# A layernorm, sliding attention and bilinear GLU kernel: one more weight group by seven products, and attention's keys and q loaded from ScalarE's queue

## The chip, the cores and the metric

The kernel runs on one core of one Trainium2 chip. The metric is the device time of one execution in microseconds (us), as the median of several runs; lower is better. A core has TensorE (PE, the matrix products; PEld is its weight load), VectorE (DVE), ScalarE (ACT), GpSimd (POOL) and SyncE (SP). Each engine works through its own queue in order. SP, ACT and POOL can each start DMA transfers from their queue.

## The reference

```python
x = A_x                                            # 1 x 2048 x 640
xn = layernorm(x)
q, k, v = heads(xn @ wqkv)                         # 32 heads of 20
# position s looks at s, s-2, ..., s-14 (8 keys, masked below 0)
s = softmax(q . k / sqrt(20)) @ v,  then @ wo
g = silu(((xn @ w_gate) * (xn @ w_up)) @ w_down)   # 640 -> 1536 -> 640
return x + s * g
```

The code feeds one normalized, transposed x (`xT`) both to q, k, v and to gate and up.

## The kernel before

Everything on TensorE is a product of float32 numbers that are split into a high and a low part; three of the four part products are computed (`ALL3`). ScalarE makes a high part as a copy, and GpSimd or VectorE the low part as a difference (`split`, L112). So each operand that is made on the chip costs one pass on ScalarE and one on GpSimd or VectorE.

**Order of the work.** The order on each engine is that of the Python text; it is written out by hand. First come x, its norm and its transpose into `xT` (4 chunks of 512 positions, each a high and a low part of 5 rows of 128). Between these stand the products for q, k, v of the first unit and gate and up of weight groups 0 and 1. There are 12 weight groups of 128 columns, f = 0 to 11. For groups 0 and 1 all chunks are computed in the plain form: `gate_up(f, ch)` is 30 products of 512 columns, 15 for gate and 15 for up.

Then q, k, v follow for the rest of the heads (`qkv(m, r, i)`, L426): five sets of heads m = 0 to 4, two residues r, eight row tiles i, 15 products each. The result of a tile goes to a PSUM bank. While attention runs, the banks come from `ring = [q_one, "g", "u"]` (L517): bank q has one buffer, g and u have two each. ScalarE copies the bank out (L448), and every second tile a DMA writes it to `scr` in DRAM (L452), from ScalarE's queue for m > 0 and from SP's for m = 0.

**Attention** (L468) runs beside this on VectorE and GpSimd. It is a Python generator; `advance(budget)` (L623), called behind each piece of TensorE work, emits as much of it as the budget covers (0.38 a head behind each tile of q, k, v; 0.184 a product in the groups). It works through 12 units (heads of a group, residue) in the order of `ORDER`. For each unit VectorE multiplies q by keys (L542) and sums over a head (L549); the softmax follows; and for the values VectorE multiplies (L508) while GpSimd adds (L514). `ahead` (L480) asks for the next unit's keys and q (`load_kq`, L409) from the middle of the unit before, if they have been written, and for its values (`load_kv`, L417) in the unit itself. All of these loads are in SP's queue.

**Seven products.** From group `F_TWO` = 2 to group 10 the plain form is replaced (`group`, L1253). For two chunks at once, gate and up of 4 of the 5 rows are treated as a 2 x 2 block product by Strassen's scheme in Winograd's form, with seven block products in place of eight; the fifth row is added plainly. `group(f, 2)` is for chunks 2 and 3, `group(f, 0, 1)` for chunks 0 and 1. In the order of the code the seven have 6, 9, 6, 9, 6, 9 and 9 matrix products of 512 columns. This takes:
- sums of x: for chunks 2 and 3 by `differences` (L1156), on GpSimd in steps beside q, k, v; for chunks 0 and 1 by `early_sums` and `early_high` (L598, L611), early, stored to DRAM and loaded back by `load_t` and `load_e` (L1145, L1150) from GpSimd's queue;
- sums of weights on GpSimd (`w_add`, L1229), and splits (`w_split`, L1215) into the tiles G, S, R and U, where U is kept in the rear of R's buffer. For group f + 1 they are made while group f runs, at the places listed in `two_places` (L1410). They start from `wf_raw[f + 1]`, loaded by SP (`load_wf`, L178) into one of two buffers `wraw`; the sums `w_sum[f]` use the other.

At the end of q, k, v (L1391 to L1394) the rest of the steps is emitted, R of the first such group is split, and the next group's raw weights are loaded. Then come groups 2 to 10, group 11 with the output projection between its parts, the projection's remaining products, and the down projection (L866).

Of the kernel before, what the change touches and what calls it, by code (L numbers as in the profile page):

```python
# [42 lines left out]
NP = NT // 2  # L43
PAIRS = range(0, W, 2)
PACE = 1.0
VEC = 2
EARLY = 1
GROUP_RATE = 0.184

# [7 lines left out]
def kernel(  # L57
# [120 lines left out]
    def load_wf(f):  # L178
        wf_raw[f] = slot([P, KD, 2, P], F32) if f == 0 else st([P, KD, 2, P], "wraw", 2)
        nc.sync.dma_start(wf_raw[f], wgu[f])  # L180
# [228 lines left out]
    def load_kq(u):  # L409

        c, b = GROUPS[UN[u][0]] * DH, ORDER.index(u) % 2
        view_kv(u, b)
        q_t[u] = st([P, NE, c], "q", 1)
        nc.sync.dma_start(q_t[u], scr[u][:, 0])
        load_kv(u, 0)

    def load_kv(u, a):  # L417

        zero_kv(u, ORDER.index(u) % 2, a)
        nc.sync.dma_start(kv_t[u][:, a, W - 1:, :], scr[u][:, 1 + a])  # L420
        for p0, p1 in ((0, 112), (112, 127)):
            nc.sync.dma_start(kv_t[u][p0 + 1:p1 + 1, a, 0:W - 1, :], scr[u][p0:p1, 1 + a, 1:, :])

    ALL_RUNS = [(a, b, k) for a, b in ALL3 for k in range(KD)]

# [688 lines left out]
    gate_up(0, 2)  # L1114
    trans_q(15)
    low_parts()
    early_high(1)
    for a in range(2):
        nc.sync.dma_start(e_scr[2 + a], xT[3][a][:, 0:2, :].bitcast(F32))
    made.add(0)  # L1120
# [1 line left out]
    for i in range(TPC, NE):  # L1122
        qkv(0, 1, i)
        advance(PACE * 1.9)
    split_wq(1, nc.gpsimd)
    gate_up(1, 2)
    gate_up(0, 3)
    gate_up(1, 3)

    f0, f1 = KF - 2, KF - 1  # L1130
    F_TWO = 2
    tt, tw, steps = {0: [], 2: []}, {}, []
    T_UNIT = {(j, a, k): divmod(n, 3) for n, (j, a, k) in
              enumerate((j, a, k) for k in range(2) for j in ("T1", "T2", "T3") for a in range(2))}
# [10 lines left out]
    def load_t(n):  # L1145

        tt[0].append(slot([P, 3, CH]))
        nc.gpsimd.dma_start(tt[0][n], t_scr[:, 3 * n:3 * n + 3])
# [104 lines left out]
    def group(f, c0=0, second=0):  # L1253

        b = {"A": pt([P, CH], "g", 2), "C": pt([P, CH], "u", 2), "B": q_one}
        kept, later = {}, []
        eng = nc.vector if c0 and f >= VEC else nc.gpsimd

        def hold(j):
            kept[j] = st([P, CH], "gh", 5)  # L1260
            nc.scalar.activation(kept[j], b["ACACABA"[j]], AF.Copy)  # L1261

        def gate_b():
            nc.vector.tensor_add(kept[2], kept[2], b["C"])

        def up_b():
            eng.tensor_add(kept[1], kept[1], kept[4])

        def h_b():
            eng.tensor_mul(kept[2], kept[2], kept[1])  # L1270
            store_h(f, c0 + 1, kept[2])

        def gate_a():
            nc.vector.tensor_add(kept[0], kept[0], b["B"])

        def up_a():
            nc.vector.tensor_mul(kept[0], kept[0], b["A"])
            store_h(f, c0, kept[0])

        if not second:  # L1280
            if not two(f - 1):
                w_split(f, "U")
            w_sum.pop(f, None)
            wf_raw.pop(f)
        for n, j in enumerate((0, 5, 2, 1, 4, 3, 6)):
            y = b["ACACABA"[j]]
            runs = [(w_unit(f, H_IN[j], k)[i], x_in(W_IN[j], l, k, c0)) for i, l in ALL3 for k in range(2)]
            if j in FIVE:
                name, ch = FIVE[j]
                runs += [(w_unit(f, name)[i], xT[c0 + ch][l][:, KD - 1, :]) for i, l in ALL3]  # L1290
            for r, (w, x) in enumerate(runs):
                nc.tensor.matmul(y, w, x, start=j in (0, 1, 5) and r == 0, stop=r == len(runs) - 1,  # L1292
                                 skip_group_check=True)
            if j in (0, 1, 2, 4):
                hold(j)
            finish_piece()
            if (second, n) == (1, 6) and (second, n) in places:
                places.pop((second, n))(f)
            for act in later:
                act()  # L1300
            later = {5: [gate_a], 3: [gate_b, up_b] + [h_b] * (eng is nc.gpsimd)}.get(j, [])
            if j == 6:
                unfinished.extend([up_a] + [h_b] * (eng is nc.vector))
            if (second, n) in places:
                places[second, n](f)
            if (f, second, n) in beside:
                beside[f, second, n]()
            if (second, n) == (0, 0) and f < f1 and f + 1 not in wf_raw:
                load_wf(f + 1)
            advance(PACE * len(runs) * (GROUP_RATE if two(f) else 0.184))  # L1310
# [32 lines left out]

    def first_parts():
        for name in ("S1", "S2", "S3", "d5", "S4"):
            w_add(2, name)
            yield
        w_split(2, "S")
        yield

    steps += [differences(k) for k in range(2)]
# [4 lines left out]
    for m, t in ((m, t) for m in range(1, len(MADE)) for t in range(DIL)):  # L1356
        r = t if m < last else DIL - 1 - t
        begin_unit(m, r)
        heads, broad = MC[m] // DH, m < last and MC[m + 1] > CMAX
        for i in range(NE):  # L1360
            n = t * NE + i
            if m < last and n == 0:
                load_wq(m + 1, ((0, 2), (2, 4)) if broad else ((0, 3), (3, 5)))
            elif m < last and n in BLOCK:
                split_wq(m + 1, nc.gpsimd, (BLOCK.index(n), BLOCK.index(n) + 1))
            elif broad and n == BLOCK[1] + 1:
                load_wq(m + 1, ((4, 5),))
            if (m, r, i) == (last - 1, 1, 6):
                load_wf(2)
            if (m, n) in W_SUMS:  # L1370
                wd_sum(W_SUMS.index((m, n)))
            qkv(m, r, i)
            if m == last and n == NT - 7:
                staged[:] = [y for y in staged if y is not stage_pk[-1]]
            elif m == last and n == NT - 5:
                load_t(0)
            elif m == last and n == NT - 3:
                w_split(2, "G")
            if i == 1:
                finish_piece()  # L1380
            advance(PACE * heads * 0.38)
            paced += RATE[m - 1][t]
            while paced >= 1:
                paced -= 1
                step()
        if (m, r) == (last - 1, 1):
            steps.append(first_parts())
        elif (m, r) == (last, 1):
            for k in range(2):
                last_difference(k)  # L1390
    step(100)  # L1391
    w_split(2, "R")
    w_sum.pop(2)
    load_wf(3)  # L1394
    beside.update({(f0, 0, 5): lambda: advance(1e9), (f0, 1, 0): lambda: begin_last(), (f0, 1, 1): lambda: load_pair(0),
                   (f0, 1, 4): lambda: sums_wo(), (f0, 1, 6): lambda: split_wo(0, nc.vector)})

# [6 lines left out]
    def sums(*names):  # L1404
        return lambda f: w_add(f + 1, *names)

    def splits(*names):
        return lambda f: w_split(f + 1, *names)
# [8 lines left out]
            load_e(1, 0, 0)  # L1417
            load_e(1, 1, 1)

    for f in range(2, f1):  # L1420
        places.clear()
        places.update(two_places)
        if f == F_TWO:
            for n, at in enumerate((0, 2, 3, 4)):
                places[0, at] = lambda f, n=n: load_late(n)
        group(f, 2)
        group(f, 0, 1)
    places.clear()
    beside.update({(f1, 0, 0): lambda: split_wo(1, nc.vector),
                   (f1, 0, 2): lambda: (turn_pair(0), load_pair(1)), (f1, 0, 4): lambda: (hi_pair(0, 0), lo_pair(0, 0)),  # L1430
# [200 lines left out]
```

## Time and profile before

| | |
|---|---|
| median of 3 runs | 736.02 us (735.68 to 736.02) |
| the profiled execution | 736.29 us, of which the span is 734.4 us |
| products on TensorE | 4030 |
| bytes moved by DMA | 143.78 MB, mean 196 GB/s |

By stage, from the trace's table of busy time (us of each engine in a stretch of the span):

| stretch | us | PE | DVE | ACT | POOL |
|---|---|---|---|---|---|
| x, norm, first q, k, v, gate and up | 0 to 85 | 85.0 | 60.6 | 52.1 | 53.0 |
| gate_up(1, 2), (0, 3), (1, 3) | 85 to 105.4 | 20.4 | 19.0 | 5.4 | 9.5 |
| q, k, v of m = 1 to 4 | 105.4 to 272.7 | 167.3 | 142.6 | 49.0 | 139.4 |
| group 2 | 272.7 to 297.2 | 24.5 | 23.5 | 9.0 | 23.1 |
| groups 3 to 10 | 297.2 to 493.1 | 195.9 | 178.8 | 64.2 | 161.7 |
| group 11 and the output projection | 493.1 to 582 | 88.9 | 84.0 | 50.9 | 52.1 |
| down projection and the output | 582 to 734.4 | 148.1 | 118.0 | 71.6 | 11.7 |

In the profile each row names a line of the kernel, an engine, the operation and the tiles (out<-in, without buffer numbers). What stands in brackets behind a row of the timeline is the time for which the engine was idle before it, and what ended that. SPq, ACTq and POOLq are the queues' own instructions, such as the issue of a DMA.

### The profile page before, as it was taken

The numbers are of one execution on the slowest core, as the hardware profiler recorded it, in microseconds if no ns is written. First come the engines' busy times: TensorE is split into PE (matmuls) and PEld (weight loads), VectorE is DVE, ScalarE is ACT, GpSimd is POOL, SyncE is SP. The second block draws the span as 40 slices with busy tenths as digits, with TensorE's granted clock in tenths as the row PEclk, the third lists the DMA queues.
The fourth block names the chain that finished last, engine by engine and source line by source line (L and its number), as shares of the span: only waits on it lengthen the run. The fifth ranks groups of instructions, "written<-read, shape, count | busy, mean of one in ns | idle before, by whom it ended". The sixth has DMA issues, their size and how long they took to land.

```text
span 734.4 us, 11062 instructions
## 1 busy us (share of the span) xinstructions
PE 728.2 (99%) x4030; PEld 666.0 (91%) x4030; DVE 626.5 (85%) x729; ACT 302.2 (41%) x561; POOL 450.5 (61%) x383
## 2 busy tenths in 40 slices
PE   8999999999999999999999999999999999999997
PEld 6989989988999998888888888888999999999997
DVE  7676998798796989899889999969899997777775
ACT  5668312323232333333233322334566664444442
POOL 6159919997779889797879969766644550000000
PEclk9999999999999999999999999999999999999999
DMA  8564588789767669462733542376768965555534
GB/s 325 170 204 158 208 303 300 239 256 257 190 193 164 220 204 323 141 180 87 221 88 105 177 141 68 80 218 183 208 211 241 315 236 194 194 194 194 194 108 143
DMA packets 106148, 143.78 MB, mean 196 GB/s; under 512 B 23048, under 2 KB 75524, under 8 KB 106094
## 3 DMA queue, kind: packets, MB, share of 16 engines
q1 hardware_dynamic: 88366, 121.13, 52.0%
q10 hardware_dynamic: 16000, 12.78, 5.4%
q0 software_dynamic: 1728, 9.18, 5.1%
q8 instruction: 31, 0.51, 0.3%
q14 instruction: 23, 0.19, 0.1%
HBM read 94.40 MB, written 55.67 MB: 204 GB/s over the span
## 4 chain that ended last, share of the span: by engine, by line
PE 98%; DMA 1%; DVE 0%; SPq 0%; ACT 0%; issue 0%
PE g L1292 16%; PE u L1292 11%; PE q L434 11%; PE q L866 9%; PE u L434 8%; PE g L434 8%; PE u L866 6%; PE q L1292 5%; PE u L124 5%; PE g L124 5%; PE q L996 3%; PE g L866 3%; PE e L866 3%; PE u L996 2%; PE e L996 2%; PE g L996 1%
## 5 line engine op out<-in xcount | busy, mean ns | idle before, releaser
L514 POOL TENSOR_TENSOR o<-o,t 128x960 f32<-128x960 f32 (+1 forms) x66 | 133.7, 2025 | 11.3 <-DVE t L508 10.1
L508 DVE TENSOR_TENSOR t<-e,kv 128x960 f32<-128x960 f32 (+1 forms) x96 | 99.6, 1038 | 21.1 <-POOL o L514 21.1
L542 DVE TENSOR_TENSOR t<-q,kv 128x1920 f32<-128x1920 f32 (+1 forms) x48 | 92.4, 1926 | 2.8 <-DMA kv<-qkv_scr 2.7
L549 DVE TENSOR_REDUCE lg<-t 128x96 f32<-128x1920 f32 (+1 forms) x48 | 92.3, 1923 | 0.2
L434 PE MATMUL q<-s,xc 128*128 128x360 f32 (+1 forms) x450 | 82.8, 334 | 0.5 <-DVE lg L272 0.5
L1261 ACT ACTIVATE gh<-g 128x512 f32<-128x512 f32 x57 | 34.2, 600 | 109.0 <-PE g L1292 108.1
L434 PEld LDWEIGHTS q<-s,xc 128*128 128x128 f32 x450 | 74.8, 188 | 4.6 <-DVE lg L272 0.7
L115 POOL TENSOR_TENSOR s<-wraw,s 128x384 fp32r<-128x384 f32 (+6 forms) x57 | 68.0, 1209 | 17.5 <-ACT s L114 17.5
L434 PE MATMUL u<-s,xc 128*128 128x360 f32 (+1 forms) x360 | 65.8, 334 | 0.0
L434 PEld LDWEIGHTS u<-s,xc 128*128 128x128 f32 x360 | 60.3, 188 | 2.3
L434 PE MATMUL g<-s,xc 128*128 128x360 f32 (+1 forms) x330 | 61.5, 337 | 0.0
L434 PEld LDWEIGHTS g<-s,xc 128*128 128x128 f32 x330 | 55.7, 188 | 2.6
L1292 PE MATMUL g<-s,s 128*128 128x512 f32 x228 | 57.9, 389 | 0.0
L1292 PE MATMUL u<-xc,s 128*128 128x512 f32 x228 | 57.9, 389 | 0.0
L866 PE MATMUL q<-xc,s 128*128 128x320 f32 x342 | 55.5, 309 | 0.0
L866 PEld LDWEIGHTS q<-xc,s 128*128 128x128 f32 x342 | 51.5, 188 | 0.0
L1292 PEld LDWEIGHTS g<-s,s 128*128 128x128 f32 x228 | 42.8, 188 | 8.9
L1292 PEld LDWEIGHTS u<-xc,s 128*128 128x128 f32 x228 | 42.8, 188 | 8.9
L114 ACT ACTIVATE s<-wraw 128x384 fp32r<-128x384 f32 (+6 forms) x58 | 32.6, 581 | 29.4 <-PE g L1292 10.2
L1292 PE MATMUL q<-xc,pk 128*128 128x512 f32 x171 | 41.9, 389 | 0.0
L1292 PE MATMUL g<-xc,s 128*128 128x512 f32 x171 | 41.9, 389 | 0.0
L514 POOL TENSOR_TENSOR o<-t 128x960 f32<-128x960 f32 (+1 forms) x11 | 22.1, 2011 | 27.4 <-DVE t L508 22.7
(328 smaller groups left out, 1559.7 us busy)
## 6 DMA issues: line engine op xcount, KB each, us to landing
h_scr<-gh SPq DMA_DIRECT2D x48, 256.0 KB, 2.8
wraw<-in_wgu SPq DMA_DIRECT2D x11, 640.0 KB, 4.8
kv<-qkv_scr SPq DMA_DIRECT2D x14, 480.0 KB, 6.1
t<-h_scr SPq DMA_DIRECT2D x8, 768.0 KB, 6.3
qkv_scr<-s ACTq DMA_DIRECT2D x17, 360.0 KB, 4.4
kv<-qkv_scr SPq DMA_DIRECT2D x14, 367.5 KB, 7.1
s_scr<-gh SPq DMA_DIRECT2D x16, 320.0 KB, 3.6
gh<-s_scr SPq DMA_DIRECT2D x16, 320.0 KB, 4.1
```

The costliest lines, as they stand in the source:

```text
L114: nc.scalar.activation(hi, raw, AF.Copy)
L115: eng.tensor_sub(lo, raw, hi.bitcast(F32))
L124: nc.tensor.matmul(acc, a, b, start=first and n == 0, stop=last and n == len(runs) - 1)
L434: nc.tensor.matmul(p, xT[(r * NE + i) // TPC][a][:, k, t0:t0 + P], wq[m][b][k], start=n == 0, stop=n == len(runs) - 1, skip_group_check=ac ...
L508: nc.vector.tensor_mul(t.rearrange("p (n d) -> p n d", d=DH), e[:, :, w].unsqueeze(2).to_broadcast([P, NE * nh, DH]), v)
L514: return NE * c * cost, lambda: eng.tensor_add(y, z, t)
L542: nc.vector.tensor_mul(t, q, k)
L549: nc.vector.tensor_reduce(out=lg[:, :, j:j + 2].rearrange("p n a -> p a n"), in_=t.rearrange("p a (n d) -> p a n d", d=DH), op=ALU.add, ax ...
L866: nc.tensor.matmul(p, y[:, i, k], wd_part(name, k, l), start=new and r == 0, stop=r == len(runs) - 1, skip_group_check=True)
L996: nc.tensor.matmul(b, y, w, start=new and r == 0, stop=r == len(runs) - 1, skip_group_check=True)
L1261: nc.scalar.activation(kept[j], b["ACACABA"[j]], AF.Copy)
L1292: nc.tensor.matmul(y, w, x, start=j in (0, 1, 5) and r == 0, stop=r == len(runs) - 1, skip_group_check=True)
```

## The change

- `F_TWO` goes from 2 to 1 and `VEC` from 2 to 1. Chunks 2 and 3 of group 1 are no longer computed by gate_up(1, 2) and gate_up(1, 3); `group(1, 2)` does it, as the first of the groups. Chunks 0 and 1 of group 1 stay in the plain form.
- The raw weights of group 1 are loaded a second time, and the weight sums and splits that were made for group 2 beside q, k, v are now made for group 1. Those of group 2 are made within `group(1, 2)`, at the places of `one_places`, which has them all in one half.
- Keys and q of the next unit are loaded from ScalarE's queue until the end of q, k, v, and from SP's after that. Values stay with SP.
- In the second half of unit (0, 1), behind tile 5: the split of wq for m = 1, the load of wq for m = 2, and `early_high(1)`, in this order. Before, early_high(1) came ahead of tile 4, the split behind tile 7 and the load at the start of m = 1.
- `load_t(0)` and `load_t(1)` move from the last row tiles and group 2 to group 1's first places; `load_t(2)`, `load_t(3)` and `load_e` to places of group 2.
- The pace of attention beside q, k, v goes from 0.38 to 0.39 a head.

```diff
-VEC = 2
+VEC = 1
...
-        nc.sync.dma_start(q_t[u], scr[u][:, 0])
-        load_kv(u, 0)
-
-    def load_kv(u, a):
+        by[0].dma_start(q_t[u], scr[u][:, 0])
+        load_kv(u, 0, by[0])
+
+    by = [nc.scalar]
+
+    def load_kv(u, a, eng=nc.sync):
 
         zero_kv(u, ORDER.index(u) % 2, a)
-        nc.sync.dma_start(kv_t[u][:, a, W - 1:, :], scr[u][:, 1 + a])
+        eng.dma_start(kv_t[u][:, a, W - 1:, :], scr[u][:, 1 + a])
         for p0, p1 in ((0, 112), (112, 127)):
-            nc.sync.dma_start(kv_t[u][p0 + 1:p1 + 1, a, 0:W - 1, :], scr[u][p0:p1, 1 + a, 1:, :])
+            eng.dma_start(kv_t[u][p0 + 1:p1 + 1, a, 0:W - 1, :], scr[u][p0:p1, 1 + a, 1:, :])
...
     gate_up(0, 2)
     trans_q(15)
     low_parts()
-    early_high(1)
...
     for i in range(TPC, NE):
         qkv(0, 1, i)
         advance(PACE * 1.9)
-    split_wq(1, nc.gpsimd)
-    gate_up(1, 2)
+        if i == TPC + 1:
+            split_wq(1, nc.gpsimd)
+            load_wq(2, ((0, 2), (2, 4)))
+            early_high(1)
     gate_up(0, 3)
-    gate_up(1, 3)
+    wf_raw.clear()
 
-    F_TWO = 2
+    F_TWO = 1
...
-            if (second, n) == (1, 6) and (second, n) in places:
+            if n == 6 and (second, n) in places and (second or f == F_TWO):
                 places.pop((second, n))(f)
...
     def first_parts():
         for name in ("S1", "S2", "S3", "d5", "S4"):
-            w_add(2, name)
+            w_add(F_TWO, name)
             yield
-        w_split(2, "S")
+        w_split(F_TWO, "S")
...
-            if m < last and n == 0:
-                load_wq(m + 1, ((0, 2), (2, 4)) if broad else ((0, 3), (3, 5)))
-            elif m < last and n in BLOCK:
+            if 1 < m < last and n == 0:
+                load_wq(m + 1, ((0, 3), (3, 5)))
+            if m < last and n in BLOCK:
...
-                load_wf(2)
+                load_wf(F_TWO)
...
-            elif m == last and n == NT - 5:
-                load_t(0)
             elif m == last and n == NT - 3:
-                w_split(2, "G")
+                w_split(F_TWO, "G")
...
-            advance(PACE * heads * 0.38)
+            advance(PACE * heads * 0.39)
...
+    by[0] = nc.sync
     step(100)
-    w_split(2, "R")
-    w_sum.pop(2)
-    load_wf(3)
+    w_split(F_TWO, "R")
+    w_sum.pop(F_TWO)
+    load_wf(F_TWO + 1)
...
-    for f in range(2, f1):
+    one_places = {(0, 2): splits("G"), (0, 3): sums("S1", "S2", "S3"), (0, 4): splits("S"),
+                  (0, 5): lambda f: (w_add(f + 1, "d5", "S4"), w_split(f + 1, "R")), (0, 6): splits("U")}
+    for f in range(F_TWO, f1):
         places.clear()
-        places.update(two_places)
+        places.update(two_places if f > F_TWO else one_places)
         if f == F_TWO:
-            for n, at in enumerate((0, 2, 3, 4)):
+            places[0, 0] = lambda f: load_t(0)
+            places[0, 1] = lambda f: load_t(1)
+        elif f == F_TWO + 1:
+            for n, at in enumerate((0, 2, 4), 1):
                 places[0, at] = lambda f, n=n: load_late(n)
         group(f, 2)
-        group(f, 0, 1)
+        if f > F_TWO:
+            group(f, 0, 1)
```

## The prediction

> **What bounds the kernel now.** I read the page first, then the waits of TensorE, then the chain of waits in order of time.
>
> ```profile
> span 734.4 us, 11062 instructions
> PE 728.2 (99%) x4030; PEld 666.0 (91%) x4030; DVE 626.5 (85%) x729; ACT 302.2 (41%) x561; POOL 450.5 (61%) x383
> ...
> PE 98%; DMA 1%; DVE 0%; SPq 0%; ACT 0%; issue 0%
> ```
>
> ```profile
> PE q L229 <- POOL lg masks.py:199: 1.4, 1, 1.4
> PE q L434 <- DVE lg L272: 0.5, 1, 0.5
> ```
>
> The span is 734.4 us of an execution of 736.29, so 1.89 us lie around it; the median of the runs shown, 736.02, is 0.27 below this execution. TensorE is busy for 99% of the span, the chain that ended last is TensorE for 98% of it, and TensorE's two waits, for the identity and for the first norm, stand at the very start. So a product less is time less, and any new wait of TensorE is time more. Nothing else counts by itself: the question is only what makes TensorE wait.
>
> ```profile
> 85.17 3.40 PE g L124 x15
> ...
> 478.80 3.40 PE g L1292 x15
> ```
>
> The chain gives the prices: 15 products of 512 columns take 3.40 us, in the plain form (L124) as in the seven-product form (L1292), so 0.2267 us each.
>
> **What is taken away.** gate_up(1, 2) and gate_up(1, 3) are 2 x 30 = 60 products. group(1, 2) is 6+9+6+9+6+9+9 = 54. Six products at 0.2267 are 1.36 us, gained wherever TensorE stays packed. It is also the most that the change can gain, 0.185%. About 0.2% (1.47 us) is what a measurement of this kernel can tell from no change.
>
> **What is moved: the end of unit (0, 1).** Taking out the two gate_ups brings `qkv(1, 0, 0)` 13.6 us forward, to just behind gate_up(0, 3). The keys and q of attention unit 1 are now asked for on ScalarE's queue, in the middle of gate_up(0, 3), right behind ScalarE's copy of the gate. They read what `qkv(0, 1, 7)` wrote to DRAM, and that write stays on SP. So the first question is when it lands; the rows of before around it, from the timeline and the DMA view:
>
> ```profile
> 80.61 1.30 POOL L608 TENSOR_TENSOR kv<-kv,xc 128x512 f32<-128x512 f32 x1
> 81.85 0.61 POOL L616 CAST kv<-kv 128x512 fp32r<-128x512 f32 x1
> 85.00 3.56 PE L124 MATMUL g<-xc,s 128*128 128x512 f32 x15
> 88.35 1.30 POOL L617 TENSOR_TENSOR kv<-kv,t 128x512 fp32r<-128x512 f32 x1
> 89.61 4.39 POOL L115 TENSOR_TENSOR s<-wraw,s 128x1080 fp32r<-128x1080 f32 x3
> 90.09 0.88 SPq L1119 DMA_DIRECT2D e_scr<-xc  x2
> 91.94 1.19 SPq L452 DMA_DIRECT2D qkv_scr<-pk  x1
> 96.41 0.33 SPq L414 DMA_DIRECT2D q<-qkv_scr  x1
> 97.26 0.91 SPq L422 DMA_DIRECT2D kv<-qkv_scr  x2
> 105.40 2.56 PE L434 MATMUL q<-s,xc 128*128 128x360 f32 x15
> 108.00 0.47 ACT L448 ACTIVATE s<-q 128x360 f32<-128x360 f32 x1 [5.20 <-PE q L434]
> 112.60 2.56 PE L434 MATMUL q<-s,xc 128*128 128x360 f32 x15
> ```
>
> ```profile
> qkv_scr<-pk SPq DMA_DIRECT2D x1, 360.0 KB, 4.4
> ```
>
> ```profile
> DMA to landing us min/median/max: 3.0/4.4/12.3
> ```
>
> The second fence is that one write; the third is all the writes of q, k, v (L452) from 85 to 150 us. Step by step:
>
> 1. GpSimd ends the early sums at 81.91 as before. The split of wq(1) (4.39) now comes first, to 86.30; then early_high(1), which took from 81.85 to 89.65 = 7.80, to 94.10.
> 2. SP has early_high's eight stores ahead of the write of `qkv(0, 1, 7)`, so that write goes out at about 94.5 instead of 91.94.
> 3. It landed in 4.4, behind a megabyte of e_scr<-xc and its sister write. Those now go some 10 us earlier, so I take 3.4, nearer to the shortest, 3.0; both ends are kept. Landed: 97.9.
> 4. ScalarE issues the four loads (from 96.41 to 98.17 on SP: 1.76), to 99.7; evacuates `qkv(1, 0, 0)` (0.47, the row at 108.00), to 100.1.
> 5. TensorE is through gate_up(0, 3) at 85.00 + 6.80 = 91.8, fills q, g and u, and wants bank q again three tiles later, as from 105.40 to 112.60, which is 7.2: at 99.0. It stalls 1.1 us; with a landing in 3.0 it is 0.7, in 4.4 it is 2.1. The 12.3 would make it 10, and I leave it out: of the rows it is the furthest from a quiet queue.
>
> That ScalarE does stand still behind a DMA of its own queue is in the trace:
>
> ```profile
> 151.10 4.39 ACTq L452 DMA_DIRECT2D qkv_scr<-pk  x2
> 155.54 0.57 ACT L448 ACTIVATE s<-q 128x480 f32<-128x480 f32 x1 [4.46 <-DMA wraw<-in_wqkv]
> ```
>
> Its two writes held the queue for 4.39 us, and the next evacuation began only at 155.54. The Trainium skill (DMA: Bandwidth & Descriptors, Anatomy of one DMA) says the same of waits: any semaphore wait is spent on the issuing sequencer, before dispatch. Its fit there, 2.0 us plus bytes over 436 GB/s, would land 360 KB in an estimated 2.8 us, for a stall of 0.5 and 0.6 us less in the sum; the trace has nothing under 3.0, and its row is used. Against the change, the skill (Trainium Kernel Development and Optimization, Key Constraints) has it that issuing from several engines saves issue time only.
>
> Later units are safe: by the paces written in the code (an advance of 0.39 a head against 0.38) each next unit was written at least two tiles of q, k, v before its load is asked for, and its loads wait for nothing but 1.8 us of issue on an engine that is busy for 41%.
>
> **What is added: group 1 gets weights of its own form.** wgu[1] is loaded a second time (at nothing: SP asks for it at the place where it asked for wgu[2], two tiles ahead of the first sum), and five sums and four splits are made for it, by the steps that made group 2's. What is new is that group 2's must be made within half a group, mostly by GpSimd:
>
> ```profile
> L514 POOL TENSOR_TENSOR o<-o,t 128x640 f32<-128x640 f32 x24 | 38.2, 1592 | 3.1 <-DVE t L508 2.7
> L115 POOL TENSOR_TENSOR s<-wraw,s 128x384 fp32r<-128x384 f32 x19 | 20.6, 1097 | 0.2 <-ACT s L114 0.2
> L115 POOL TENSOR_TENSOR s<-wraw,s 128x768 fp32r<-128x768 f32 x10 | 18.5, 1855 | 6.8 <-ACT s L114 6.8
> L1238 POOL TENSOR_TENSOR wraw<-wraw 128x256 f32<-128x256 f32 x20 | 18.0, 900 | 14.5 <-DMA wraw<-in_wgu 14.5
> L1238 POOL TENSOR_TENSOR wraw<-wraw,wraw 128x256 f32<-128x256 f32 x20 | 16.1, 803 | 0.5
> L115 POOL TENSOR_TENSOR pk<-wraw,pk 128x640 fp32r<-128x640 f32 x10 | 15.8, 1575 | 3.9 <-ACT pk L114 3.9
> L1238 POOL TENSOR_TENSOR wraw<-wraw 128x128 f32<-128x128 f32 x10 | 6.1, 614 | 0.0
> ```
>
> ```profile
> 109.50 2.27 POOL L514 TENSOR_TENSOR o<-t 128x960 f32<-128x960 f32 x1 [14.80 <-DVE t L508]
> ...
> 272.60 1.52 PE L1292 MATMUL g<-xc,pk 128*128 128x512 f32 x6
> 273.87 0.94 ACT L114 ACTIVATE s<-wraw 128x384 fp32r<-128x384 f32 x2 [0.60 <-ACT s L448]
> 276.24 2.02 POOL L115 TENSOR_TENSOR s<-wraw,s 128x384 fp32r<-128x384 f32 x2
> 277.30 0.35 SPq L180 DMA_DIRECT2D wraw<-in_wgu  x1
> ```
>
> ```profile
> wraw<-in_wgu SPq DMA_DIRECT2D x11, 640.0 KB, 4.8
> ```
>
> The sums of one group are 2 x 0.90 + 2 x 0.80 + 0.61 = 4.02, its splits 1.58 (G) + 1.86 (S) + 2 x 1.10 (R, U) = 5.63: 9.65 us of GpSimd. They can't start before wgu[2] is there, whose buffer comes free with the R split of group 1: in group 2 of before that load went out at 277.30, 4.70 after the group's start at 272.60, and 4.8 later the weights are there: 9.5. That R split came late only because GpSimd was behind; ScalarE's half of it was there at 273.87 + 0.47. Straight behind that, with 1.0 for it, the load goes out 2.9 after the start and lands at 7.7. The last thing made is U, and its low part is wanted by the 30th product of group 2: 12.24 + 29 x 0.2267 = 18.81. So GpSimd has 11.1 us for 9.65, and attention's additions (1.59 each) stand between: with none U is 1.5 early, with one 0.13 late, with two 1.7, with three 3.3; with the load at 9.5, 1.8 more. I take no backlog and one addition, 0.13: GpSimd's one long idle time, 14.80 us before 109.50, now holds the first steps of the sums for chunks 2 and 3, and an addition that is due before 7.7 runs in time which is idle anyhow. Ends for the range: 0 and 3.5.
>
> VectorE gets four passes more for group 1, hidden in its 15% of idle time unless attention's end slips (third rival); ScalarE's extra copies go into its 59%. The first chunks' sums, loaded later, are read in the second half of group 2; the last of them is asked for behind 8.2 us of group 2 and read behind 22.4, and these 14 us hide it unless GpSimd's queue is late by most of them. I put it at nothing.
>
> **The sum.** 736.29 - 1.36 + 1.13 + 0.13 = 736.19 on this execution; 0.27 less for the median: 735.9. That is no change; with a landing in 3.0 or 4.4 this case runs from 735.5 to 736.9.
>
> **The rivals.** (a) No new wait reaches TensorE: the write lands early, or GpSimd is quicker through early_high(1), and U is in time. Then all 1.36 us are kept: 734.7. For it: 0.7 us is a short stall; against it: SP's order of stores before the write is fixed in the code.
> (b) GpSimd has too much in group 1's half: it arrives with group 2's backlog and one addition, or without it and with two, and U is 1.7 to 1.9 late. 735.9 + 1.8 = 737.7, slower; each further addition is 1.6 more. It decides from the second addition on. For it: VectorE starts unit 1 later (its keys are asked for 1.5 us later), so its products and GpSimd's additions come later too.
> (c) VectorE is late at the end of attention:
>
> ```profile
> 478.03 0.68 DVE L1274 TENSOR_TENSOR gh<-gh,q 128x512 f32<-128x512 f32 x1
> ```
>
> Bank q of group 10 is read out at 478.71, and by the chain it is wanted again at 478.80 + 15 x 0.2267 = 482.2: 3.5 us of slack. VectorE's added 2.9 us (estimated: four passes between 0.68 and 1.2 for the group, less two of 0.68 for the plain form) and 1.36 us of earlier products would make it 0.8 late, beside the stall at 99: 736.7.
> That the change does not do what it says can be left out: the count of products is written in the code.
>
> **How the numbers follow.** Forecast 0.35, (a) 0.27, (b) 0.29, (c) 0.09. The bounds of 0.2% are 734.55 and 737.49. (a) stands 0.1 inside the first, and the runs shown lie 0.34 apart: two fifths of it, 0.11, are faster. Slower are (b) and the late ends of the forecast and of (c): 0.36. The rest is the same: 0.53. The range takes in (a) with its scatter, and (b) with one addition more: 734.5 to 739.3.
>
> **What would show it.** TensorE has 4024 products. Right: a gap of about 1.1 us before the fourth tile of m = 1, put down to ScalarE's copy, with ScalarE idle behind loads on its own queue from 89 us; wgu[2] issued about 3 us behind group 1's start; no gap over 0.5 us in group 2. Rival (a): no gap between 85 and 300 us. Rival (b): a gap in group 2's fourth product, put down to GpSimd's split. Wrong altogether: TensorE waits somewhere else, or has a slower product.

## The result

The changed kernel takes 757.69 us (median of 4 runs, 754.39 to 758.49) beside 736.02 for the kernel before: a ratio of 1.0287, with a 95% interval of 1.0256 to 1.0317. The change costs 21.7 us. Its profiled execution took 757.7 us, with a span of 755.9, against 736.29 and 734.4 before.

The page of the changed kernel, the lines that answer to those of before:

```profile
span 755.9 us, 11062 instructions
...
PE 736.1 (97%) x4024; PEld 668.8 (88%) x4024; DVE 622.8 (82%) x731; ACT 305.9 (40%) x568; POOL 457.5 (61%) x392
...
PE 74%; POOL 9%; DMA 7%; DVE 4%; issue 3%; ACT 1%; SPq 1%; ACTq 0%; POOLq 0%; DVEq 0%
```

The six products are gone (4024). But TensorE is no longer the whole chain: a quarter of it now runs over GpSimd, DMAs and VectorE, although none of them became much busier. The waits of TensorE in the changed kernel (total us, how often, the longest):

```profile
PE g L1295 <- ACT gh L1264: 5.9, 3, 3.7
PE g L1295 <- POOL pk L115: 4.3, 2, 3.1
PE q L436 <- ACT s L450: 1.9, 2, 1.0
PE u L1295 <- ACT gh L1264: 1.9, 2, 1.1
```

(L1295 are the groups' products, L1292 before; L436 those of q, k, v, L434 before. L450 and L1264 are ScalarE's copies out of PSUM.) The timeline of TensorE shows where:

```profile
96.09 2.56 PE L436 MATMUL u<-s,xc 128*128 128x360 f32 x15
99.70 2.74 PE L436 MATMUL q<-s,xc 128*128 128x360 f32 x15 [1.04 <-ACT s L450]
102.28 2.63 PE L436 MATMUL g<-s,xc 128*128 128x360 f32 x15
...
115.63 2.74 PE L436 MATMUL q<-s,xc 128*128 128x360 f32 x15 [0.86 <-ACT s L450]
...
263.96 1.55 PE L1295 MATMUL g<-xc,pk 128*128 128x512 f32 x6
...
268.91 1.66 PE L1295 MATMUL g<-s,s 128*128 128x512 f32 x6 [1.33 <-ACT gh L1264]
...
275.09 2.34 PE L1295 MATMUL u<-xc,s 128*128 128x512 f32 x9 [1.12 <-ACT gh L1264]
...
286.60 2.93 PE L1295 MATMUL g<-s,s 128*128 128x512 f32 x6 [3.74 <-ACT gh L1264]
...
313.27 1.20 PE L1295 MATMUL g<-xc,pk 128*128 128x512 f32 x2 [3.05 <-POOL pk L115]
```

A half group is one call of `group`, 54 products; packed, it takes 12.24 us, so the starts of the halves make a ledger. The two gate_ups are gone (60 x 0.2267 = 13.6), and at 85 us this execution was 0.5 ahead of that of before (84.50 for 85.00), so group 1 was due at 272.60 - 13.6 - 0.5 = 258.5.

| where | lost, us | how it comes out |
|---|---|---|
| q, k, v | 5.5 | group 1 starts at 263.96, not 258.5 |
| group 1, and groups 2 and 3 | 13.4 | halves of 15.34, 17.61 and 17.18 (the third is the first half of group 3) |
| halves that start between 387 and 440 | 4.5 | four of 13.50, 12.71, 13.37 and 13.86 |

23.4 lost, less the 1.36 of the products and the lead of 0.5, make 21.5: the difference of the spans.

**In q, k, v.** ScalarE and SP in the changed kernel (ACTq and SPq rows are DMA issues):

```profile
93.99 0.53 SPq L454 DMA_DIRECT2D qkv_scr<-pk  x1
...
96.93 0.35 ACTq L414 DMA_DIRECT2D q<-qkv_scr  x1
...
97.90 1.23 ACTq L424 DMA_DIRECT2D kv<-qkv_scr  x2
99.18 0.47 ACT L450 ACTIVATE s<-q 128x360 f32<-128x360 f32 x1 [10.48 <-PE u L436]
...
100.04 0.58 ACTq L454 DMA_DIRECT2D qkv_scr<-s  x1
...
115.11 0.47 ACT L450 ACTIVATE s<-q 128x360 f32<-128x360 f32 x1 [6.03 <-DMA qkv_scr<-s]
```

The first stall is the predicted one: the write out at 93.99, the loads behind it to 99.13, the copy after them. 99.70 is 1.2 later than the three tiles before allow. The second was not predicted: the write issued at 100.04 landed only after 15.0 us, beside four transfers of w_d of 960 KB each and the load of the next wq, and ScalarE had to wait before it could use the buffer that this write read (6.03 us, the last row). And from 99.70 on each tile of 360 columns takes 2.467 us in place of 2.40, until q, k, v end: 45 x 0.067 = 3.0 us with no wait at all.

**In groups 1 to 3.** GpSimd, ScalarE and SP there:

```profile
266.40 0.99 ACTq L424 DMA_DIRECT2D kv<-qkv_scr  x2
268.85 2.00 POOL L115 TENSOR_TENSOR s<-wraw,s 128x384 fp32r<-128x384 f32 x2
269.90 0.36 SPq L180 DMA_DIRECT2D wraw<-in_wgu  x1
271.43 1.59 POOL L516 TENSOR_TENSOR o<-o,t 128x640 f32<-128x640 f32 x1
273.55 1.56 POOL L516 TENSOR_TENSOR o<-o,t 128x640 f32<-128x640 f32 x1
276.60 0.73 POOL L1241 TENSOR_TENSOR wraw<-wraw 128x256 f32<-128x256 f32 x1
278.80 2.03 POOL L516 TENSOR_TENSOR o<-o,t 128x640 f32<-128x640 f32 x1
284.20 0.94 ACT L114 ACTIVATE s<-wraw 128x384 fp32r<-128x384 f32 x2 [4.47 <-POOL wraw L1241]
285.97 0.58 ACT L1264 ACTIVATE gh<-g 128x512 f32<-128x512 f32 x1
287.25 1.00 POOL L115 TENSOR_TENSOR s<-wraw,s 128x384 fp32r<-128x384 f32 x1
289.11 0.83 SPq L180 DMA_DIRECT2D wraw<-in_wgu  x1
```

wgu[2] is asked for at 269.90, 5.9 us behind the group's start. Its last low part (287.25) ends at 288.2, where the products wanted it at 263.96 + 18.81 = 282.8. Between 265.16 and 287.3 GpSimd has six of attention's additions to do. The first gap, before 268.91, is another matter: from 265.22 to 267.39 ScalarE issues four loads of a next unit's keys and q (266.40 are the last two), and its copy for TensorE comes only behind them and a split, at 268.28. In group 2, ScalarE's copy out of the bank (285.97) stands in the queue behind a split that waited 4.47 us for GpSimd's sums; that is why the trace puts the gap before 286.60 down to ScalarE. Then wgu[3] goes out at 289.11 and takes 13.9 us to land, which makes the gap before 313.27.

### The profile page after: what moved, and what is told of

It is laid out like the page before. It is cut to its first block, busy times and chain, and to the rows that moved or that the text cites. A ratio compares the mean times of both kernels' runs of the same rounds, so it can differ in the third digit from the quotient of the medians.

```text
span 755.9 us, 11062 instructions
## 1 busy us (share of the span) xinstructions
PE 736.1 (97%) x4024; PEld 668.8 (88%) x4024; DVE 622.8 (82%) x731; ACT 305.9 (40%) x568; POOL 457.5 (61%) x392
## 4 chain that ended last, share of the span: by engine, by line
PE 74%; POOL 9%; DMA 7%; DVE 4%; issue 3%; ACT 1%; SPq 1%; ACTq 0%; POOLq 0%; DVEq 0%
PE g L1295 11%; PE q L868 8%; PE q L436 7%; PE u L1295 7%; PE u L436 6%; PE g L436 6%; PE u L868 6%; PE q L1295 4%; PE q L998 3%; PE g L868 3%; PE e L868 3%; DMA wraw<-in_wgu 2%; PE u L998 2%; PE g L124 2%; POOL kv L610 2%
## 5 line engine op out<-in xcount | busy, mean ns | idle before, releaser
L436 PE MATMUL q<-s,xc 128*128 128x360 f32 (+1 forms) x450 | 84.3, 337 | 2.1 <-ACT s L450 1.9
L1264 ACT ACTIVATE gh<-g 128x512 f32<-128x512 f32 x60 | 36.0, 599 | 119.4 <-PE g L1295 117.8
L436 PEld LDWEIGHTS q<-s,xc 128*128 128x128 f32 x450 | 75.6, 188 | 7.0 <-ACT s L450 2.5
L115 POOL TENSOR_TENSOR s<-wraw,s 128x384 fp32r<-128x384 f32 (+6 forms) x60 | 73.1, 1233 | 14.4 <-ACT s L114 14.3
L1295 PE MATMUL g<-s,s 128*128 128x512 f32 x240 | 62.5, 397 | 5.1 <-ACT gh L1264 5.1
L436 PE MATMUL u<-s,xc 128*128 128x360 f32 (+1 forms) x360 | 66.8, 337 | 0.0
L1295 PE MATMUL u<-xc,s 128*128 128x512 f32 x240 | 61.7, 392 | 1.9 <-ACT gh L1264 1.9
L436 PEld LDWEIGHTS u<-s,xc 128*128 128x128 f32 x360 | 61.2, 188 | 2.3
L436 PE MATMUL g<-s,xc 128*128 128x360 f32 (+1 forms) x330 | 62.4, 340 | 0.0
L1295 PEld LDWEIGHTS g<-s,s 128*128 128x128 f32 x240 | 45.7, 191 | 15.4 <-ACT gh L1264 5.9
L436 PEld LDWEIGHTS g<-s,xc 128*128 128x128 f32 x330 | 56.5, 188 | 2.6
L1295 PEld LDWEIGHTS u<-xc,s 128*128 128x128 f32 x240 | 44.8, 188 | 13.0 <-ACT gh L1264 3.1
L114 ACT ACTIVATE s<-wraw 128x384 fp32r<-128x384 f32 (+6 forms) x61 | 34.6, 584 | 48.7 <-issue 12.9
L1295 PE MATMUL q<-xc,pk 128*128 128x512 f32 x180 | 45.3, 397 | 0.0
L1295 PE MATMUL g<-xc,s 128*128 128x512 f32 x180 | 44.2, 390 | 0.8 <-ACT gh L1264 0.8
L1241 POOL TENSOR_TENSOR wraw<-wraw 128x256 f32<-128x256 f32 (+1 forms) x33 | 24.0, 733 | 32.2 <-DMA wraw<-in_wgu 32.2
```

The lines of the kernel that those rows point to most:

```text
L114: nc.scalar.activation(hi, raw, AF.Copy)
L115: eng.tensor_sub(lo, raw, hi.bitcast(F32))
L436: nc.tensor.matmul(p, xT[(r * NE + i) // TPC][a][:, k, t0:t0 + P], wq[m][b][k], start=n == 0, stop=n == len(runs) - 1, skip_group_check=ac ...
L1241: nc.gpsimd.tensor_tensor(v[name], v[a], v[b], op=ALU.add if name == "S1" else ALU.subtract)
```

## The experiments

Two theories stood against each other. **The queue**: ScalarE's in-order queue is what fails; loads and splits that wait stand ahead of copies out of PSUM. **The crowd**: GpSimd has not the time to make group 2's weights in half a group, and whatever queue one relieves, the gap comes back elsewhere. The kernel before, timed beside them, took 735.87 to 736.21. Behind each time stands, in brackets, the 95% interval of its ratio to the kernel before.

**1. Keys and q from SP's queue again, in the changed kernel**

```diff
-    by = [nc.scalar]
+    by = [nc.sync]
```

> The changed kernel with one part undone: keys and q are loaded from SP's queue throughout. Theory A (loads that wait on ScalarE's own queue hold the copies out of PSUM behind them): the stalls before the tiles at 99.70 and 115.63 us (1.2 and 1.0) and the 360-column tiles of 2.467 us in place of 2.40 behind them (45 tiles, 3.0) go, and about 1 us of the stall at 268.91: 757.7 - 6.2 = 751.5, from 750.5 to 753. Theory B (the earlier place of m = 1 is what hurts: the write of the last tile of unit (0, 1) and the DMA traffic are late whatever queue loads): the stalls stay, 756 to 758.

755.25 (1.024 to 1.0283). Both stalls in m = 1 are gone and all its tiles take 2.40, so they did come from ScalarE's queue; the gap in group 1 before its third set of products (268.91 in the changed kernel) is gone too. But TensorE waits 0.72 before 185.57, where ScalarE, by the trace, had waited 8.39 us for one of its own writes, and from there the tiles take 2.467 again: group 1 starts at 262.15, only 1.8 earlier. Groups 1 to 3 lose 11.1. A holds for the place, not for the sum.

**2. The seven products alone**: as run 1, with unit (0, 1) in its old order (early_high(1) ahead of tile 4, the split behind tile 7, the load of wq for m = 2 at the start of m = 1) and the old pace.

```diff
+    early_high(1)
...
-        if i == TPC + 1:
-            split_wq(1, nc.gpsimd)
-            load_wq(2, ((0, 2), (2, 4)))
-            early_high(1)
+    split_wq(1, nc.gpsimd)
...
-            advance(PACE * heads * 0.39)
+            advance(PACE * heads * 0.38)
```

> The kernel before with the seven products for group 1 alone: unit (0, 1) in the old order, keys and q from SP's queue, pace 0.38; group 2's weights made within group 1, and the first chunks' sums loaded at the changed places. Theory A (two separate causes; the one of groups 1 to 3 is the crowded half group: splits on ScalarE that wait for GpSimd's sums, with copies out of PSUM behind them, and wgu[3] late): the gaps of the changed kernel at 268 to 327 us stay, 12 to 16 us, less the 1.4 of the six products: 747 to 751. Theory B (group 1 was late only since attention and the queues came late out of the disturbed q, k, v): no gap over 1.5 us in groups 1 to 3, 735 to 738.

751.08 (1.0171 to 1.0239), at the end of A's range. Groups 1 to 3 lose 11.1 (halves of 19.20, 13.32 and 15.29) with no load on ScalarE's queue, so those loads do not explain them; splits that wait on ScalarE are still there, and run 5 is about these. Group 3 loses 3.0 of the 11.1 although its weights landed in 4.2 us, so their late landing is not the only way to lose there. And q, k, v lose 5.5 here too (group 1 starts at 264.53, where 259.0 was due): TensorE waits 0.47 before 94.09 for GpSimd's split of wq, and from 95.18 on the tiles take 2.467. ScalarE's loads are thus not the only thing that makes q, k, v late at the earlier place.

**3. ScalarE's loads alone, in the kernel before**

```diff
-        nc.sync.dma_start(q_t[u], scr[u][:, 0])
+        by[0].dma_start(q_t[u], scr[u][:, 0])
```

Here `by[0]` is ScalarE's queue until the end of q, k, v, then SP's, for the keys too.

> The kernel before with keys and q loaded from ScalarE's queue until the end of q, k, v, and nothing else. Theory A (a load on ScalarE's queue costs only where its write has not landed when TensorE is about to need ScalarE): at unit 1 two gate and up pieces lie between the write and the next need, no stall over 0.3 us there, 736.0 to 737.0, and the 360-column tiles stay at 2.40. Theory B (any such load delays the copies by its issue of about 2 us, in every unit): stalls at several units and slow tiles behind the first of them, 739 to 742.

744.67 (1.0106 to 1.014), worse than either theory. Nothing happens at unit 1, as A has it, but the unit after it costs one long wait. ScalarE and TensorE in this run:

```profile
129.62 0.63 ACT L1168 ACTIVATE s<-gh 128x512 fp32r<-128x512 f32 x1 [6.94 <-POOL gh L1164]
130.16 0.45 ACT L450 ACTIVATE s<-g 128x360 f32<-128x360 f32 x1
130.64 0.52 ACTq L454 DMA_DIRECT2D qkv_scr<-s  x1
134.91 0.35 ACTq L414 DMA_DIRECT2D q<-qkv_scr  x1
137.27 0.45 ACT L450 ACTIVATE s<-u 128x360 f32<-128x360 f32 x1
138.13 3.77 PE L436 MATMUL q<-s,xc 128*128 128x360 f32 x15 [3.96 <-ACT s L450]
```

The load stands right behind the write that it reads, so ScalarE waits out its landing. They are that close because ScalarE came late to the write: it had waited 6.94 us for one of GpSimd's sums for chunks 2 and 3. The same wait is in the kernel before, where it cost nothing:

```profile
129.19 0.63 ACT L1166 ACTIVATE s<-gh 128x512 fp32r<-128x512 f32 x1 [6.32 <-POOL gh L1162]
```

So ScalarE, at 41%, had no slack at this place. The wait (4.1), the slow restart of the next tiles (1.8) and then 2.467 a tile (30 x 0.067 = 2.0) make the 8 us by which group 2 starts later.

**4. One wait of TensorE, in the kernel before**

```diff
+            for _ in range(12 if (m, r, i) == (1, 0, 0) else 1):
                 nc.scalar.activation(y[...], p..., AF.Copy)
```

> The kernel before, where ScalarE copies the first tile of m = 1 out of its bank twelve times over in place of once (the same values), so that TensorE has to wait once, for about 0.8 us, before the fourth tile; nothing else differs. Theory A (one wait of TensorE leaves the 360-column products in a slower rhythm until products of another kind reset it): all 360-column tiles behind it take 2.467 us, 44 x 0.067 = 2.9 more, so 736.0 + 0.8 + 2.9 = 739.7. Theory B (the slow tiles come from the DMA traffic or from where the operands lie): the tiles go back to 2.40 at once, 736.8.

741.05 (1.0055 to 1.0085): A in kind, and 1.35 more than its number.

```profile
110.15 2.56 PE L434 MATMUL u<-s,xc 128*128 128x360 f32 x15
114.00 2.74 PE L434 MATMUL q<-s,xc 128*128 128x360 f32 x15 [1.29 <-ACT s L449]
116.58 2.63 PE L434 MATMUL g<-s,xc 128*128 128x360 f32 x15
```

The wait of 1.4 us made group 2 start 4.8 later. No DMA was added, and no operand lies elsewhere.

**5. Group 2's high copies by GpSimd, in the changed kernel**

```diff
+            if f == F_TWO + 1:
+                nc.gpsimd.tensor_copy(hi, y)
+                nc.gpsimd.tensor_sub(lo, y, hi.bitcast(F32))
```

> The changed kernel, where the high copies of group 2's splits are made by GpSimd in place of ScalarE; nothing else differs. Theory A (ScalarE's queue: a split that waits for GpSimd's sum or for the load of wgu[2] holds the copies out of PSUM behind it): the gaps before 275.09 and 286.60 us (1.3 and 3.9, both put down to ScalarE's gh) go, and GpSimd, with some 3 us more to do, makes U later by as much, of which 1 to 3 reach TensorE: 757.7 - 5.2 + 2 = 754.5, from 752 to 756. Theory B (GpSimd simply has too little time in the half group, and it does not matter who makes the high parts): the gaps move to GpSimd's low parts and grow by its added work, 758 to 761.

756.79 (1.025 to 1.0289). ScalarE's waits in group 2 are gone, but TensorE's waits have moved:

```profile
PE u L1300 <- POOL s L1232: 2.6, 1, 2.6
PE g L1300 <- ACT gh L1269: 2.1, 2, 1.3
...
PE g L1300 <- POOL s L1232: 1.4, 1, 1.4
```

(L1232 is GpSimd's new copy.) The gap went where B has it: group 2's first half now loses 7.9 in place of 5.4, near the 3 us that GpSimd got to do more. But group 1's half loses 1.7 in place of 3.1, as A has it, and group 3 only 0.8, so that groups 1 to 3 lose 10.3 in place of 13.4; q, k, v were 1.9 later in this execution, and the total hardly moved. So ScalarE's queue has a part in group 1, and in group 2 the gap stays whichever engine makes the high copies.

**6. Without group 2's weights, in the changed kernel**

```diff
-    load_wf(F_TWO + 1)
...
-        places.update(two_places if f > F_TWO else one_places)
+        places.update(two_places if f > F_TWO else {})
```

> The changed kernel without the making of group 2's weights: they are not loaded, summed or split, and group 2 computes with group 1's (so its columns are not those of the reference). Theory A (the crowded half group is the cause of all gaps from 275 to 327 us): those before 275.09 and 286.60 (1.3 and 3.9), the slower clock behind the second (1.3), the late wgu[3] with its gap (3.4) and the slow stretch behind it (1.2) go, 11.1 in all: 757.7 - 11.1 = 746.6, from 745 to 749. Theory B (the gaps come from attention and the queues, which leave q, k, v late): most of them stay, over 752.

747.96 (1.0141 to 1.0171): A. The half of group 1 takes 13.88, and the three behind it 12.24 each. The crowd costs 13.4 - 1.6 = 11.8 us; 2.3 of that was taken back by longer stalls in q, k, v in this execution (group 1 at 266.23). The 1.6 that stay are the gap behind ScalarE's four loads, which run 1 does not have.

**7. The first chunks' sums loaded early, in the changed kernel**

```diff
+            elif m == last and n == NT - 5:
+                load_t(0)
...
+            for n, at in enumerate((0, 2, 3, 4)):
+                places[0, at] = lambda f, n=n, act=places.get((0, at)): (load_late(n), act and act(f))
```

> The changed kernel with the first chunks' sums loaded at the places of before: the first from GpSimd's queue five tiles ahead of the end of q, k, v, the others and the two chunk parts in group 1's places 0, 2, 3 and 4, so that none is left in group 2. Theory A (the 13.9 us that wgu[3] took to land come from the 2.6 MB of sums loaded beside it in group 2): it lands in 5 to 7 us, the gap before 313.27 us (3.4) and the slow stretch behind it (1.2) go, 753 to 754. Theory B (it lands late for other traffic, or group 1's half gets as much worse): 757 to 760.

755.4 (1.0246 to 1.0279). The load of wgu[3], in the table of DMA issues (count, KB, median us to landing), first in the changed kernel from 287 us on, then in this run from 280 on:

```profile
wraw<-in_wgu SPq DMA_DIRECT2D x1, 640.0 KB, 13.9
```

```profile
wraw<-in_wgu SPq DMA_DIRECT2D x1, 640.0 KB, 5.2
```

It lands in time and group 3 is packed, which wins 4.9: A, for the cause. But group 2 loses 7.6 in place of 5.4 and group 1 3.4 in place of 3.1, so half of it was given back.

**8. One wait, and a few wide products behind it, in the kernel before**

```diff
+        if (m, r, i) == (1, 0, 6):
+            for _ in range(4):
+                nc.tensor.matmul(wide_p, xT[0][0][:, 0, :P], xT[0][0][:, 0, :], start=True, stop=True)
```

> The kernel before with one stall (ScalarE copies the first tile of m = 1 out twelve times, as in the run that took 741.05) and, ahead of the seventh tile of m = 1, four added products of 512 columns whose result is thrown away. Theory A (wide products put TensorE back into the quick rhythm): the tiles behind them take 2.40 us again, 741.05 + 0.9 - 38 x 0.067 = 739.4. Theory B (only a much longer or other stretch does): the tiles stay at 2.467, 741.9.

742.23 (1.0064 to 1.0097). In the profiled execution, 739.90, the tiles behind the wide products take 2.40 again: A. The three others took 742.2 to 742.4, near what B expects, and no trace shows their tiles. So the rhythm can be changed there, but not surely; this stays open.

**9. Attention stands still in group 1, in the changed kernel**

```diff
+            if f != F_TWO:
                 advance(PACE * len(runs) * (GROUP_RATE if two(f) else 0.184))
```

> The changed kernel, where attention stands still during group 1 (its budget there is nothing; the units go on behind it). Theory A (GpSimd has no time in the half group because attention's additions fill it: six of them, 9.7 us, from 265.16 to 287.29): of the 11.1 us lost from 275 to 327 at most 3 stay, and the total falls to 749, unless attention, now some 12 us later, ends too late and gives a part back at groups 10 and 11 (then 750 to 757, with the gaps there). Theory B (the late load of wgu[2] and ScalarE's waits do it, whatever GpSimd has to add): over 5 us of gaps stay from 275 to 300.

749.51 (1.016 to 1.0217): A. GpSimd in this run makes all of group 2's sums and splits with no addition between them (the first split, the last, and the first addition behind):

```profile
273.17 1.55 POOL L115 TENSOR_TENSOR pk<-wraw,pk 128x640 fp32r<-128x640 f32 x1 [2.62 <-ACT pk L114]
...
281.94 1.98 POOL L115 TENSOR_TENSOR s<-wraw,s 128x384 fp32r<-128x384 f32 x2 [0.63 <-ACT s L114]
...
284.45 1.59 POOL L516 TENSOR_TENSOR o<-o,t 128x640 f32<-128x640 f32 x1
```

Groups 1 to 3 lose 4.9 in place of 13.4. wgu[2] still comes late (asked for at 268.50, 6.1 behind the group's start), so that a wait of 1.41 is left in group 2; and attention, now behind, holds TensorE for 2.47 at 500.05. Group 3 is packed here, for wgu[3] is asked for at 282.97, 0.9 ahead of the first chunks' sums, and lands in 4.6 us; in the changed kernel it is asked for 0.9 behind two of them.

**10. Run 2 without group 2's weights** (the edit of run 6)

> The seven products for group 1 alone (old order of unit (0, 1), keys and q from SP's queue, pace 0.38), and without the making of group 2's weights: group 2 computes with group 1's (its columns are not those of the reference). Theory A (the crowded half costs here what it cost in the changed kernel, 9.7 us): 751.1 - 9.7 = 741.4. Theory B (only the gaps that this version shows in groups 1 to 3 go, 7 us by its own profile): 744.

739.62 (1.0038 to 1.01), its runs from 737.5 to 747.0; the profiled one was 737.9 and kept 2.40 a tile. A for the crowd: groups 1 to 3 lose 0.8 where run 2 loses 11.1. The other 4.9 between the two profiled executions lie in q, k, v, where both have the same code: here too TensorE waits 0.48 for the split of wq, but the tiles behind it stay at 2.40. So part of the difference between the two medians is this scatter. With group 2's weights for nothing, no load on ScalarE and unit (0, 1) in its old order, no run of this kernel was under 737.5, still over the kernel before.

**11. The old pace, in the changed kernel** (0.38 for 0.39)

> The changed kernel with the pace of attention beside q, k, v at 0.38 a head as before. Theory A (the pace set where attention stands in the groups, and so the gaps before 396.82, 437.17 and 441.71 us, 3.4 together): they go, 754.3, if the rest is the same. Theory B (it does nothing to them, or to the rest): 757.0 to 758.5.

756.24 (1.026 to 1.0294). The three late gaps go, and one comes at another half (13.59), so that the late halves lose 1.35 in place of 4.5; but q, k, v lose 3.3 more, and groups 1 to 3 11.8. Neither theory as stated: in these executions, what the higher pace costs late, it wins early. The other runs agree for the late halves: with 0.38 (runs 2 and 10) they lose 1.2 and 1.4, with 0.39 (runs 1, 5, 6, 7) 3.9 to 4.6.

**12. The kernel before without the two gate_ups**

```diff
-    gate_up(1, 2)
     gate_up(0, 3)
-    gate_up(1, 3)
```

> The kernel before without gate_up(1, 2) and gate_up(1, 3), and without anything in their place: chunks 2 and 3 of group 1 are not computed (group 0's result is stored there), so q, k, v come 13.6 us earlier. Everything else is as before. Theory A (the 13.6 us were cover for GpSimd's split of wq, for attention and for the DMAs, so that some stalls of 1 to 1.5 us in all appear in q, k, v, and the slower rhythm of the 360-column tiles, 2.7, behind the first): 736.0 - 13.6 + 4 = 726.4. Theory B (the earlier place costs nothing by itself): 722.4 to 723.

748.74 (1.016 to 1.0194), both theories missed: 60 products less made the kernel 12.5 us slower. Q, k, v and the groups behind lose about as A has it and more (group 2 starts at 264.79 where 259.0 was due, and its halves lose 4.0). The bulk is elsewhere, in the timeline of ScalarE and TensorE:

```profile
496.93 0.60 ACT L1261 ACTIVATE gh<-u 128x512 f32<-128x512 f32 x1 [13.16 <-DVE gh L1267]
497.57 2.93 PE L1292 MATMUL u<-xc,s 128*128 128x512 f32 x6 [11.89 <-ACT gh L1261]
```

Each gate_up also gave attention 6.5 us of budget. Without these 13 us the same work is emitted in one lump at the end (`advance(1e9)`, in group 10). VectorE works through it until 495.55, ScalarE's copy waits for VectorE, and TensorE for the copy. So the work taken out of the early stage was paying for attention. The changed kernel pays otherwise: 54 x 0.184 = 9.9 in group 1 and, from the higher pace, 16 tiles x 26 heads x 0.01 = 4.2. It has no gap there; runs 2 and 11, with group 1's 9.9 alone, have none either.

## Why the prediction was wrong

- **The products, and the first stall: right.** 4024 products; the write out at 93.99 (94.5 predicted), landed by 96.9 (97.9), the loads 2.2 us (1.76), a stall of 1.2 (1.13), put down to ScalarE's copy.
- **"Later units are safe": wrong.** It counted tiles in the code between a unit's write and its load, and took ScalarE for free since it is busy for 41%. Run 3 shows a load right behind its write, on a ScalarE that had just waited 6.9 us, for 8.8 us in all; in the changed kernel the loads from 265.22 on cost 1.3 us before 268.91 (run 1 has no gap there). The Trainium skill, as the prediction cites it (DMA: Bandwidth & Descriptors, Anatomy of one DMA), has a wait spent on the issuing sequencer; the 4.3 us between the issues at 130.64 and 134.91 agree. The prediction had the rule, and used it only for the one load that it looked at.
- **The long landing that was left out came.** 12.3 us was called the furthest row from a quiet queue, and it was dropped. A write of the same line and size took 15.0 here, and made the second stall. The fit of the Trainium skill (DMA: Bandwidth & Descriptors, Anatomy of one DMA), which that page gives for DMAs from GpSimd's queue, makes it an estimated 2.8; the write at 93.99, from SP's queue, was that quick, since ScalarE's loads go out 2.9 behind it, and the one at 100.04, from ScalarE's queue and beside the transfers of w_d, was not. The measurements decide.
- **What a wait costs: not in the sum.** The stall was priced at its length. In the changed kernel the tiles behind it cost 3.0 more; in run 4, 1.4 us of wait cost 4.8.
- **"I take no backlog and one addition": this step failed most.** Six additions stood between the group's start and the split of U. Two of them, and ScalarE's four loads ahead of its half of the R split, held that split up, so that wgu[2] was asked for 5.9 behind the group's start, not 2.9 (2.7 by the prediction's own rows: 1.27 + 0.47 + 1.0); it landed at 9.8 (ScalarE's first split of it is at 273.81), not 7.7; and the rest of one (273.55) and two more (278.80, 285.75) came behind that. The prices given with it were fair: 9.8 + 9.65 + 1.25 + 2.03 + 1.54 = 24.3, and U was there at 24.3 (288.2), 5.4 late in place of 0.13. Run 9, which takes the additions away, wins 8.5 of 13.4 back; run 6, which takes the work away, 11.8. The row that told it was there: GpSimd busy for 23.1 of 24.5 us in group 2, where the same making of weights had twice the time.
- **"ScalarE's extra copies go into its 59%": wrong as to where, not as to how much.** They waited, and held the copies out of PSUM behind them; run 5 takes them off ScalarE, and groups 1 to 3 still lose 10.3.
- **The first chunks' sums "at nothing": wrong.** Behind two of them wgu[3] took 13.9 us; run 7 has 5.2 without them, and run 9 has 4.6 where it is asked for ahead of them.
- **The pace: not in the sum.** The prediction used 0.39 a head only to date the loads. By runs 2, 10 and 11 the late halves lose about 3 us less with 0.38, though run 11 gives that back in q, k, v.
- **The rivals.** What happened is (b), GpSimd overloaded in group 1's half, and not at 1.8 us but at 13.4 over three groups. Its largest gap stood in group 2 as said, though under ScalarE's name and at the third product, not the fourth. (c) did not come.

Open: why the four halves from 387 to 440 lose 4.5. Run 11 shows that the pace moves these gaps. The trace of the changed kernel has, ahead of the copies for which TensorE waits before 396.82 and 437.17, ScalarE's exponential of the softmax (394.87 and 435.21), which had waited 1.77 and 1.62 us for VectorE, and a copy of the next q; the gap left in run 11 has the same two rows ahead of it. That this is the cause no run shows by taking it away.

## What to carry to other kernels

A low busy share of an engine that works in order is no slack: read what it waits for at the very place, and put nothing that waits for a DMA or a slower engine ahead of its copies out of PSUM. Where work is moved into a shorter window, list everything that the engine will have queued between the arrival of the data and the first use, other streams included, instead of pricing the new work alone. And look at what a removed piece was paying for, such as another stream's budget, before its time is booked as gain.

## What was not expected of the hardware

**Two rhythms of TensorE.** The same products of 360 columns ran at 2.40 or 2.467 us for 15, both at a granted clock of 1.00. The rhythm changed only behind a wait or a piece of other products, and either way. Run 11 came from the slow to the quick one:

```profile
237.76 2.63 PE L436 MATMUL u<-s,xc 128*128 128x360 f32 x15
241.31 2.67 PE L436 MATMUL q<-s,xc 128*128 128x360 f32 x15 [0.93 <-ACT pk L450]
243.82 2.56 PE L436 MATMUL g<-s,xc 128*128 128x360 f32 x15
```

The tile behind the wait took 2.51 (243.82 - 241.31) where the slow rhythm came to an end, and 2.58 where it began or went on (102.28 - 99.70 above). Run 7 had a wait before 101.53 and stayed quick, and run 10 one before 93.81, where run 2, with the same code there, turned slow. Tiles of 480 columns took 3.25 in both. What picks the rhythm is open.

**Half the clock behind some waits.** Busy time by stretch in the changed kernel, and then in run 7 (stretch, length, busy time and count for PE, PEld, DVE, ACT and POOL, then the granted clock, DMA share, GB/s):

```profile
286.60:289.30 2.70, 2.70 (x6) 2.17 (x7) 2.70 (x4) 0.00 (x0) 2.70 (x4) 0.50 0.42 107
289.30:292.00 2.70, 2.70 (x13) 2.19 (x12) 2.70 (x4) 0.92 (x2) 0.36 (x2) 0.98 0.96 186
```

```profile
101.50:105.60 4.10, 4.07 (x15) 4.07 (x16) 1.58 (x3) 2.61 (x5) 1.31 (x2) 0.59 1.04 427
105.60:120.00 14.40, 14.40 (x92) 14.40 (x91) 9.53 (x7) 3.62 (x7) 7.61 (x6) 1.00 1.03 370
```

Behind 286.60 six products took 2.7 us in place of 1.36, so that wait cost a third more than its length. In run 7 a wait of 2.5 us was enough, in run 5 one of 2.25 (before 101.02, clock 0.58); in run 6 one of 2.4 (before 101.35) was not. So the length alone does not decide. The Trainium skill (TensorE: Matmul & The Clock Gate, Part 1: The HAM clock gate) has the clock fall to one half after an idle window of about 3.4 us, counted by a free-running clock. The 0.50 agrees; the waits of 2.25 and 2.5 us are shorter than such a window, and the measurements stand.
